# Moving one rounded copy of the activation from ScalarE to GpSimd in an attention and two-MLP kernel

## The chip, the cores and the metric

The kernel runs on one core of a Trainium2 chip. The metric is the device time of one execution in microseconds (us). The kernel before takes 946.75 us, the median of 3 runs (946.28 to 947.42). The core has five engines, each with its own queue worked off in order: TensorE (PE, with its weight loads shown as PEld), VectorE (DVE), ScalarE (ACT), GpSimd (POOL) and SyncE (SP), which issues the transfers.

## The reference

Attention with a window of 128 positions (4 batches, 8 heads, 576 positions, 64 dimensions a head), whose result, as 2304 tokens of 512 numbers, goes through two MLPs of inner width 2048:

```
scores = q k^T / 8 - slope_h * |i - j|,  only for 0 <= i - j < 128
x  = softmax(scores) v                          # 2304 x 512
h  = x @ w_in                                   # first MLP
g  = h where h >= 1, 0 where h <= -1, else (h + 1)^2 / 4
x2 = g @ w_out
h  = x2 @ w_in2                                 # second MLP
g  = h * clip(h + 3, 0, 6) / 6
out = g @ w_out2
```

## The kernel before, in words

[...] So that accuracy is kept, every operand is split into a high part (the value rounded to fp32r) and a low part (what the rounding left), and a product is three matmuls: low by high, high by low, high by high. `split_hi` (line 150) makes the high part on an engine that its first argument names, `split_lo` (line 158) the low part by a subtraction. The weights come as 64-bit numbers and are turned into f32 on the chip by `Weights.conv1` to `conv3`: on ACT (lines 194 and 198 and the cast), POOL (line 197, the sign) and DVE (lines 205 and 212 and the subtraction).

The first MLP runs over blocks of tokens: three of 256 (N1), then four of 384. A block goes through 16 chunks f of the inner width. One chunk is `first` (12 matmuls into a bank h, line 659), `activate` (lines 688 to 692: DVE clips h, ACT squares, DVE takes the larger, then high and low part of g) and, two chunks later, `second` (12 matmuls that read g, line 701). In `second` the first of each three matmuls reads the high part of g, the second the low part. Blocks 0 and 1 go in halves: chunks 0 to 7 of block 0, 0 to 7 of block 1, then 8 to 15 of each; block 2 goes whole.

Attention runs between these chunks, one step of up to 128 queries per `tick`. For the first four units of tokens the scores are made in f32 (transposes at lines 469 and 470, products with v at line 506, x at line 531), for the later ones with split operands: `prep` makes kh, kl, qs (line 393 on POOL) and vs (line 159 on POOL), the probabilities are scaled on POOL (line 450), and POOL puts the transposed ones under two masks (line 488). Scores are matmuls at line 411, and DVE takes their minimum at line 441.

What runs on PE, DVE, ACT and POOL here is not in the order of the program text: the framework's scheduler orders each engine's queue from its own estimate of times, save where `tc.issue_after` binds an instruction. SP's queue keeps the order of the text. From the later part of the second MLP on, all queues keep the text's order.

In `activate` of the first MLP the engine of the high part is `HI["g"]`, which is "act": a cast at line 152. The low part is on POOL until the last block, which takes DVE.

## Time and profile before

| | |
|---|---|
| median of 3 runs | 946.75 us (946.28 to 947.42) |
| profiled execution, its own time | 946.02 us |
| its span, first to last instruction | 944.3 us |
| PE busy, PEld busy | 928.5 us (98%), 875.5 us (93%) |
| DVE busy | 659.4 us (70%) |
| ACT busy | 535.6 us (57%) |
| POOL busy | 306.8 us (32%), nearly all of it in the first half |
| granted clock of TensorE | 1.00 over the whole span |

Busy time is the time in which an engine executes something, a mean over stages that are limited by different things. POOL's 32% of the span is 80% and more of some stretches and nothing in others, so the rows below are taken by stretch. Idle time of an engine is put down to what ended it. PE's matmuls overlap, and one that is shown with 0.28 us holds the engine only until the next one starts.

### The profile page before, as it was taken

The numbers are of one execution on the slowest core, as the hardware profiler recorded it, in microseconds if no ns is written. First come the engines' busy times: TensorE is split into PE (matmuls) and PEld (weight loads), VectorE is DVE, ScalarE is ACT, GpSimd is POOL, SyncE is SP. The second block draws the span as 40 slices with busy tenths as digits, with TensorE's granted clock in tenths as the row PEclk, the third lists the DMA queues.
The fourth block names the chain that finished last, engine by engine and source line by source line (L and its number), as shares of the span: only waits on it lengthen the run. The fifth ranks groups of instructions, "written<-read, shape, count | busy, mean of one in ns | idle before, by whom it ended". The sixth has DMA issues, their size and how long they took to land.

```text
span 944.3 us, 17237 instructions
## 1 busy us (share of the span) xinstructions
PE 928.5 (98%) x5683; PEld 875.5 (93%) x5683; DVE 659.4 (70%) x1750; ACT 535.6 (57%) x1349; POOL 306.8 (32%) x575
## 2 busy tenths in 40 slices
PE   8899999999999999999999999999999999999998
PEld 6799999999999999999999999999999888898987
DVE  6998975786677677767656899958557777644443
ACT  6998854676667566666635786535333334423233
POOL 3243845787668676777710000000000000000000
PEclk9999999999999999999999999999999999999999
DMA  8858322232222212322017771004264654543431
GB/s 256 240 178 264 111 89 88 68 86 67 73 64 72 79 46 62 89 75 62 1 55 270 266 237 55 1 23 167 81 210 170 232 174 146 169 124 114 123 112 67
DMA packets 95337, 114.90 MB, mean 122 GB/s; under 512 B 8848, under 2 KB 73616, under 8 KB 95248
## 3 DMA queue, kind: packets, MB, share of 16 engines
q1 hardware_dynamic: 95248, 113.80, 38.3%
q8 instruction: 45, 0.74, 0.3%
q14 instruction: 44, 0.36, 0.1%
HBM read 88.60 MB, written 25.17 MB: 120 GB/s over the span
## 4 chain that ended last, share of the span: by engine, by line
PE 89%; DVE 5%; ACT 2%; DMA 2%; issue 1%; POOL 1%; SPq 0%; ACTq 0%; DVEq 0%; POOLq 0%
PE h L659 26%; PE acc L760 21%; PE acc L701 18%; PE y L1249 7%; PE x L1249 5%; PE s L411 4%; PE r L554 3%; PE t L470 2%; PE r L506 2%; DMA rawa<-w_in 1%; DVE r L688 1%; DVE kl L391 1%; DVE r L690 1%; DVE x L159 1%; DMA kw<-kT 1%
## 5 line engine op out<-in xcount | busy, mean ns | idle before, releaser
L659 PE MATMUL h<-x,wa 128*128 128x384 f32 (+1 forms) x1344 | 231.0, 317 | 1.4 <-DVE r L690 0.9
L701 PE MATMUL acc<-g,wa 128*128 128x384 f32 (+1 forms) x1344 | 227.4, 315 | 0.4 <-POOL g L159 0.4
L760 PE MATMUL acc<-wb,g 128*128 128x512 f32 x861 | 222.2, 393 | 0.0
L659 PEld LDWEIGHTS h<-x,wa 128*128 128x128 f32 x1344 | 206.8, 189 | 4.3 <-DVE r L690 3.4
L701 PEld LDWEIGHTS acc<-g,wa 128*128 128x128 f32 x1344 | 206.3, 189 | 0.7 <-POOL g L159 0.6
L760 PEld LDWEIGHTS acc<-wb,g 128*128 128x128 f32 x861 | 159.4, 188 | 24.9
L152 ACT CAST g<-r 128x384 fp32r<-128x384 f32 (+1 forms) x208 | 101.6, 489 | 71.4 <-DVE r L1196 37.6
L159 POOL TENSOR_TENSOR g<-r,g 128x256 fp32r<-128x256 f32 (+1 forms) x96 | 92.5, 964 | 67.7 <-ACT g L152 54.8
L689 ACT ACTIVATE r<-r 128x384 f32<-128x384 f32 (+1 forms) x112 | 53.5, 479 | 81.3 <-DVE r L688 81.0
L159 DVE TENSOR_TENSOR g<-r,g 128x384 fp32r<-128x384 f32 x112 | 62.4, 557 | 41.9 <-ACT g L152 41.6
L688 DVE TENSOR_SCALAR r<-h 128x384 f32<-128x384 f32 (+1 forms) x112 | 55.4, 495 | 44.0 <-PE h L659 37.3
L488 POOL TENSOR_SCALAR_AFFINE_SELECT tt<-dist 128x256 fp32r<-128x256 f32 (+1 forms) x176 | 76.9, 458 | 13.9 <-DVE dist L483 13.8
L690 DVE TENSOR_TENSOR r<-h,r 128x384 f32<-128x384 f32 (+1 forms) x112 | 55.8, 499 | 30.3 <-ACT r L689 28.4
L659 PE MATMUL h<-x,wb 128*128 128x384 f32 x384 | 72.5, 336 | 0.0
L659 PEld LDWEIGHTS h<-x,wb 128*128 128x128 f32 x384 | 68.2, 188 | 2.6
L445 ACT ACTIVATE p<-p,sm 128x128 f32<-128x128 f32 (+2 forms) x134 | 57.3, 430 | 20.9 <-DVE sm L441 20.5
L1194 ACT ACTIVATE r<-u 128x384 f32<-128x384 f32 x32 | 16.9, 527 | 56.2 <-DVE u L1258 56.2
L554 PEld LDWEIGHTS r<-tt,vs 128*128 128x128 f32 x304 | 44.7, 189 | 3.2 <-issue 1.4
L393 POOL TENSOR_TENSOR qs<-qr,qs 128x256 fp32r<-128x256 f32 (+2 forms) x64 | 39.4, 616 | 24.9 <-ACT qs L390 13.3
L554 PE MATMUL r<-tt,vs 128*128 128x128 f32 (+3 forms) x304 | 44.3, 262 | 1.4 <-POOL tt L488 0.9
L470 PE MATMUL t<-ident,p 128*128 128x128 f32 x134 | 38.4, 288 | 0.5 <-ACT tt L152 0.5
L1249 PE MATMUL y<-wb,w 128*128 128x384 f32 x192 | 38.7, 336 | 0.0
(161 smaller groups left out, 1554.6 us busy)
## 6 DMA issues: line engine op xcount, KB each, us to landing
w<-wd SPq DMA_DIRECT2D x88, 256.0 KB, 2.7
rawa<-w_in SPq DMA_DIRECT2D x16, 512.0 KB, 5.3
rawa<-w_out SPq DMA_DIRECT2D x16, 512.0 KB, 5.4
rawb<-w_in SPq DMA_DIRECT2D x16, 512.0 KB, 3.8
rawb<-w_out SPq DMA_DIRECT2D x16, 512.0 KB, 4.7
wd<-sum SPq DMA_DIRECT2D x32, 256.0 KB, 2.1
wd<-wb SPq DMA_DIRECT2D x24, 256.0 KB, 2.8
out<-o SPq DMA_DIRECT2D x17, 256.0 KB, 2.3
```

The costliest lines, as they stand in the source:

```text
L152: nc.scalar.copy(hi, x)
L159: engines[eng].tensor_tensor(out=lo, in0=x, in1=hi.bitcast(F32), op=ALU.subtract)
L445: nc.scalar.activation(out=pt[:, :nk], in_=pt[:, :nk], func=AF.Exp, bias=sm[:, 0:1], scale=-1.0, accum_out=None if u.whole else sm[:, 1:2])
L470: nc.tensor.transpose(ps[:, 1, :], pt[:, P:] if u.whole and has_prev else pt[:, :P], ident)
L488: nc.gpsimd.affine_select(out=u.tt[:, :, s0 + s, :m], in_=both, compare_op=ALU.is_ge, fill=0.0, base=-1 + s, pattern=[[0, 2], [sign, m]], ...
L554: nc.tensor.matmul(u.r[:, qo:qo + nq], u.vs[:, j, c, :, :].rearrange("p a d -> p (a d)"), u.tt[:, part].rearrange("p s q -> p (s q)")[:, s ...
L659: nc.tensor.matmul(ps[:, :n], self.W.w_in(a, c, f), self.x_chunk(x, b, c, n), start=(k == 0), stop=(k == 3 * KC - 1))
L688: nc.vector.tensor_scalar(out=r[:, :n], in0=ps[:, :n], scalar1=-1.0, scalar2=1.0, op0=ALU.max, op1=ALU.min)
L690: self.larger = nc.vector.tensor_tensor(out=r[:, :n], in0=ps[:, :n], in1=r[:, :n], op=ALU.max)
L701: nc.tensor.matmul(acc[i][:, o * n:(o + 1) * n], self.W.w_out(a, f)[:, e * P:(e + 1) * P], g[:, b, :n], start=(first and k == 0 and o == 0 ...
L760: nc.tensor.matmul(acc[t][:, :DM], g[:, b, tg * P:(tg + 1) * P], self.W.w_out(a, f), start=(first and k == 0), stop=(last and k == 2))
L1249: nc.tensor.matmul(ps[:, :N2], w[:, a, c * P:(c + 1) * P], self.x.operand(k, c, b), start=(start and n == 0), stop=(n == 5), skip_group_ch ...
```

## The change

In `Mlp1.activate`, where the block has 256 tokens, the high part of g is made by POOL and no longer by ACT. `split_hi` does this on POOL as a multiplication by 1 twice in one instruction (`tensor_scalar`, line 154). Blocks of 384 tokens and the second MLP stay as they are. There are 48 such chunks (3 blocks of 16).

```
-            split_hi(HI["g"], g[:, 0, :n], r[:, :n])
+            split_hi("pool" if n == N1 else HI["g"], g[:, 0, :n], r[:, :n])
             split_lo(LO[self.g_lo], g[:, 1, :n], r[:, :n], g[:, 0, :n])
```

```
def split_hi(eng, hi, x):
    if eng == "act":
        nc.scalar.copy(hi, x)
    elif eng == "pool":
        nc.gpsimd.tensor_scalar(out=hi, in0=x, scalar1=1.0, scalar2=1.0, op0=ALU.mult, op1=ALU.mult)
```

As the scheduler orders the queues, other instructions move as well. PE's queue at the first chunk of g (acc_721 and acc_722 are the banks of block 0's second product, wa_397 and wa_494 weights, s scores, p and t probabilities before and after their transpose):

```order
 L411 MATMUL s_1_549<-kw_106,qw_107 128x256
 L659 MATMUL h<-x,wa_494 128x256 x12
-L701 MATMUL acc_721<-g,wa_397 128x256 x5
+L701 MATMUL acc_721<-g,wa_397 128x256 x2
 L469 MATMUL t_0_564<-ident,p_115 128x128
 L470 MATMUL t_0_564<-ident,p_115 128x128
+L701 MATMUL acc_721<-g,wa_397 128x256
 L411 MATMUL s_0_572<-kw_106,qw_107 128x256
+L701 MATMUL acc_721<-g,wa_397 128x256
 L469 MATMUL t_1_580<-ident,p_113 128x128
 L470 MATMUL t_1_580<-ident,p_113 128x128
 L701 MATMUL acc_721<-g,wa_397 128x256
```

Attention's transposes and scores have moved ahead of most of the products that read g. PE's queue differs in this way up to the end of the first half of block 1 and at two more places in the second half of block 0; behind these it is the same.

POOL's queue at the end of the first half of block 1 (rawa are weights whose sign is made, qs and vs operands of the attention; L154 is the new copy):

```order
 L197 TENSOR_SCALAR rawa_1218<-rawa_1218 128x1024
 L159 TENSOR_TENSOR g<-r,g 128x256
 L197 TENSOR_SCALAR rawa_1277<-rawa_1277 128x1024
+L159 TENSOR_TENSOR vs_1729<-vr_103,vs_1729 128x3x64
+L154 TENSOR_SCALAR g<-r 128x256
 L159 TENSOR_TENSOR g<-r,g 128x256
 L393 TENSOR_TENSOR qs_1724<-qr_1508,qs_1724 128x256
-L159 TENSOR_TENSOR vs_1729<-vr_103,vs_1729 128x3x64 x2
+L159 TENSOR_TENSOR vs_1729<-vr_103,vs_1729 128x3x64
 L197 TENSOR_SCALAR rawa_1349<-rawa_1349 128x1024
+L154 TENSOR_SCALAR g<-r 128x256
 L159 TENSOR_TENSOR g<-r,g 128x256
```

Two copies have come in between the weight rawa_1218 and the last g shown; a third stands directly ahead of rawa_1218. One of the two subtractions for vs has moved ahead of a g.

DVE's queue at the same place (L690 is the larger of h and the square, which ends r, the input of the copy; the others are passes over weights):

```order
 L205 SCALAR_TENSOR_TENSOR ma_1702<-ma_1702,rawa_1277 128x1024
 L688 TENSOR_SCALAR r<-h 128x256
 L159 TENSOR_TENSOR wa_1699<-ma_1615,wa_1699 128x1024
+L690 TENSOR_TENSOR r<-h,r 128x256
 L212 ISA ma_1702<-rawa_1277,ma_1702 128x2048
-L690 TENSOR_TENSOR r<-h,r 128x256
 L688 TENSOR_SCALAR r<-h 128x256
```

The end of r for the last chunk of block 1's first half has moved ahead of the pass at line 212.

POOL's queue in block 2, at a head whose qs is made late (tt_3285 are masked probabilities, p_115 probabilities that are scaled):

```order
-L159 TENSOR_TENSOR vs_3067<-vr_103,vs_3067 128x2x64 x2
+L159 TENSOR_TENSOR vs_3067<-vr_103,vs_3067 128x2x64
+L154 TENSOR_SCALAR g<-r 128x256
+L159 TENSOR_TENSOR vs_3067<-vr_103,vs_3067 128x2x64
 L159 TENSOR_TENSOR g<-r,g 128x256
 L488 AFFINE_SELECT tt_3285<-dist 128x2x128 x2
+L393 TENSOR_TENSOR qs_3306<-qr_3177,qs_3306 128x256
 L450 TENSOR_SCALAR p_115<-p_115,sm_0_3295 128x128
-L393 TENSOR_TENSOR qs_3306<-qr_3177,qs_3306 128x256
```

The copy has come in ahead of the low part of g, and qs has moved ahead of the scaling.

## Rows read from the trace of the kernel before

**Rows 1.** Stretches: length, then busy us of the engines, clock, DMA

```profile
core 0: us, PE busy (x) PEld busy (x) DVE busy (x) ACT busy (x) POOL busy (x), PEclk, DMA share, GB/s
40.00:83.00 43.00, 42.55 (x345) 41.21 (x344) 39.13 (x109) 40.10 (x87) 18.32 (x26) 1.00 0.57 175
83.00:107.00 24.00, 23.57 (x197) 23.13 (x197) 21.89 (x51) 22.12 (x48) 13.28 (x14) 1.00 0.72 240
107.00:133.00 26.00, 26.00 (x221) 26.00 (x220) 23.79 (x56) 17.55 (x44) 16.99 (x19) 1.00 0.24 74
133.00:160.00 27.00, 27.00 (x229) 26.92 (x228) 14.21 (x52) 12.85 (x40) 14.08 (x26) 1.00 0.36 109
160.00:228.00 68.00, 67.41 (x556) 65.86 (x556) 51.56 (x199) 46.77 (x165) 54.06 (x110) 1.00 0.26 70
```

**Rows 2.** Longest waits of PE, 40 to 228 us: total, times, longest

```profile
PE t L469 <- DVE x L159: 0.4, 1, 0.4
PE acc L701 <- POOL g L159: 0.4, 1, 0.4
```

**Rows 3.** Groups by shape, ACT and POOL, whole span: busy us, mean ns

```profile
L152 ACT CAST g<-r 128x256 fp32r<-128x256 f32 x48 | 19.5, 405 | 9.7 <-DVE r L690 8.5 <-PE s L411 0.9
...
L488 POOL TENSOR_SCALAR_AFFINE_SELECT tt<-dist 128x256 fp32r<-128x256 f32 x144 | 64.7, 470 | 13.9 <-DVE dist L483 13.8
...
L197 POOL TENSOR_SCALAR rawa<-rawa 128x1024 f32<-128x1024 f32 x16 | 23.6, 1475 | 39.5 <-ACT ma L194 22.2 <-DMA qw<-qT 8.8 <-DMA kw<-kT 4.6
...
L142 POOL TENSOR_SCALAR dist<-rel 128x256 bf16<-128x256 f32 x8 | 3.2, 406 | 0.3
```

**Rows 4.** Timeline of ACT at 97 us: start, duration, [idle before]

```profile
97.34 0.40 ACT L152 CAST g<-r 128x256 fp32r<-128x256 f32 x1
97.64 0.46 ACT L445 ACTIVATE p<-p,sm 128x192 f32<-128x192 f32 x1
...
99.82 1.20 ACT L194 ACTIVATE ma<-rawa 128x1024 f32<-128x1024 f32 x1 [0.22 <-DVE wa L159]
```

**Rows 5.** Longest wait of all engines, 25 to 230 us: total, times, longest

```profile
POOL g L159 <- ACT g L152: 27.9, 22, 3.0
```

**Rows 6.** Timeline of POOL at the first g

```profile
37.44 1.31 POOL L197 TENSOR_SCALAR rawa<-rawa 128x1024 f32<-128x1024 f32 x1 [3.91 <-DMA rawa<-w_in]
39.25 1.46 POOL L159 TENSOR_TENSOR g<-r,g 128x256 fp32r<-128x256 f32 x1 [0.49 <-ACT g L152]
```

**Rows 7.** Timeline of POOL at the end of block 1's first half

```profile
101.10 1.51 POOL L197 TENSOR_SCALAR rawa<-rawa 128x1024 f32<-128x1024 f32 x1 [0.70 <-ACT ma L194]
...
103.27 2.12 POOL L197 TENSOR_SCALAR rawa<-rawa 128x1024 f32<-128x1024 f32 x1
...
109.77 2.12 POOL L197 TENSOR_SCALAR rawa<-rawa 128x1024 f32<-128x1024 f32 x1
111.85 1.70 POOL L159 TENSOR_TENSOR g<-r,g 128x256 fp32r<-128x256 f32 x1
```

**Rows 8.** Timeline of PE at the products that read this g

```profile
113.69 1.68 PE L701 MATMUL acc<-g,wa 128*128 128x256 f32 x12
115.21 0.28 PE L659 MATMUL h<-x,wa 128*128 128x256 f32 x1
```

**Rows 9.** Timeline of DVE ahead of that

```profile
96.25 0.42 DVE L690 TENSOR_TENSOR r<-h,r 128x256 f32<-128x256 f32 x1 [0.42 <-ACT r L689]
```

**Rows 10.** Timelines of POOL and PE at a late qs in block 2

```profile
208.48 0.73 POOL L159 TENSOR_TENSOR g<-r,g 128x256 fp32r<-128x256 f32 x1
...
210.33 0.38 POOL L450 TENSOR_SCALAR p<-p,sm 128x128 f32<-128x128 f32 x1 [0.16 <-DVE sm L449]
210.67 0.74 POOL L393 TENSOR_TENSOR qs<-qr,qs 128x256 fp32r<-128x256 f32 x1
...
211.47 0.33 PE L411 MATMUL s<-kh,qs 128*128 128x128 f32 x1
```

**Rows 11.** Timelines of POOL and DVE where both read SBUF

```profile
43.95 1.17 POOL L197 TENSOR_SCALAR rawa<-rawa 128x1024 f32<-128x1024 f32 x1 [3.24 <-ACT ma L194]
...
49.34 2.21 POOL L197 TENSOR_SCALAR rawa<-rawa 128x1024 f32<-128x1024 f32 x1 [3.51 <-ACT ma L194]
...
49.32 1.21 DVE L212 CUSTOM_DVE_ANT_0 ma<-rawa,ma 128x2048 uint16<-128x2048 uint16 x1
```

**Rows 12.** Timeline of PE before the first g

```profile
38.12 0.70 PE L411 MATMUL s<-kw,qw 128*128 128x256 f32 x2 [1.09 <-DVE sm L441]
```

## The prediction

> **What bounds the kernel now.** I read the busy time by stretch first, because the change touches only the blocks of 256 tokens, whose copies of g lie between 38 and 229 us. In each stretch from 40 us on TensorE (PE) is busy for nearly all of it: it is idle for 0.45, 0.43, 0.00, 0.00 and 0.59 us, 1.47 us of 188 [rows 1]. [...] So PE bounds this part, the change takes nothing off PE, and what it can win there is first of all that 1.47 us. What it can lose is not bounded in that way: any new wait of PE comes out at the end, since the stretches behind are full too.

> Second, the helpers in the same rows. From 40 to 83 us ACT is busy for 40.10 of 43 us and DVE for 39.13; POOL only for 18.32. From 160 to 228 us it is the other way round: POOL has 54.06 of 68 us, ACT 46.77. The change moves work from ACT to POOL, which is welcome in the first stretch and unwelcome in the last.

> Third, the waits of PE: the two longest after 40 us are 0.4 us for DVE's x and 0.4 us for POOL's g [rows 2]. Neither is for the cast on ACT that the change removes.

> **The change, part by part.**

> *Removed:* 48 casts on ACT, of 405 ns [rows 3], 19.4 us of busy time. ACT starts its next instruction before a cast has ended: the one at 97.34 lasts 0.40, its successor starts at 97.64 [rows 4], so a cast takes 0.30 us of ACT's queue, 14.4 us in all.

> *Added:* 48 copies on POOL. The trace has no copy from f32 to fp32r there. The nearest rows are the same instruction on as many elements with a bf16 result, 406 ns, and a select on as many elements with an fp32r result, 470 ns; the upper end is the same instruction on four times as many elements, 1475 ns [rows 3]. I take 0.45 us, between the two of the right size: 21.6 us. In the unblocked case I see no reason for less than 0.41.

> *What hides it:* before its 48 subtractions POOL stood idle 22 times, for 27.9 us, until ACT's cast had ended [rows 5]. There the copy runs in a gap that is gone anyway, 0.45 in place of 0.41 and one hand-over fewer. The other 26 times it did not wait for ACT, so the copy is added to its queue. What follows is where that queue is tight.

> *First g, at 40 us.* PE waits 0.4 us for it [rows 2]. POOL is held until 38.75 by a weight's sign (37.44 + 1.31) [rows 6], and the subtraction starts at 39.25. A copy from 38.75 of 0.45 us lets it start at 39.20, and saves the hand-over: -0.05, call it -0.1 us at most. In the changed order PE has only two products of that g ahead of the transposes instead of five, so a late g holds up the attention a little less or the same.

> *End of block 1's first half, 101 to 114 us.* This is the tightest place. POOL works from 101.10 without any idle to the end of the subtraction at 113.55 (111.85 + 1.70) [rows 7]. The 12 products that read this g start at 113.69 and the next ones at 115.21 [rows 8], so each takes 0.13 us; the second is the first that reads the low part, and is due at 113.82. Slack: 0.27 us. By the changed POOL order one copy comes ahead of the weight at 101.10, where POOL had been idle for 0.70 us and which hides it, and two copies come between that weight and this subtraction; half of a pair of subtractions for vs goes ahead of one g, which moves nothing in the total. Two copies of 0.45 are 0.90, less the slack 0.27: 0.63 us late. Against it stands a lead: POOL's start at 101.10 follows ACT's weight pass of 99.82 [rows 4], that follows DVE, and DVE had lost 0.42 us at 96.25 waiting for ACT's square [rows 9]. The removed casts ahead of it give back one spacing, 0.30. Term: +0.3 us. Its bounds: 0 (the lead is larger, ACT being freed of 13 casts since 40 us) and +2.6 us (below).

> Behind the subtraction POOL has a qs of the attention and the next g. In the changed order DVE makes that g's maximum ahead of a weight pass and no longer behind it, so I put no second wait there.

> *Block 2, 160 to 228 us.* 16 copies of 0.45 are 7.2 us, and POOL has 13.9 us idle (68 - 54.06) [rows 1]; it stays below 91%. The one tight place that I find is the qs that ends at 211.41 (210.67 + 0.74) and is read by scores at 211.47 [rows 10]. The copy ahead of the g at 208.48 would push it by 0.45. But in the changed order this qs stands ahead of the scaling of p, so it gains 0.38 and the 0.16 us that POOL waited for DVE there. Term: 0, bounds -0.4 (the chain of DVE and ACT runs ahead because ACT is freed) and +0.9 (two copies late).

> The sum is -0.1 + 0.3 + 0 = +0.2 us. The profiled execution took 946.02 us, a span of 944.3 and 1.7 around it, so 946.2 by its own time. The median of the runs is 946.75, 0.73 above the profiled one; I forecast **947.0 us**, no measurable change. For this kernel 0.2%, or 1.9 us, is about what a measurement can tell from none.

> [...] The trace shows that copies on POOL can cost more than 0.45. A weight's sign on POOL lasts 1.17 us at 43.95 and 2.21 us at 49.34, where DVE had just begun, at 49.32, an addition of two tiles in SBUF; that addition lasted 1.21 us [rows 11]. So POOL waited for DVE, about 1.0 us. From 103 to 114 us POOL's weight passes take 2.12 us and the subtractions 1.70 again [rows 7].

> [...]

> **Rivals.**

> 1. *Slower: POOL's queue at 101 to 114 us with blocked copies.* If each of the two copies is held by DVE as the weight's sign was, it takes 0.45 + 1.0 = 1.45 us; two are 2.9, less the slack 0.27: +2.6 us, 949.4 us. It decides from 1.25 us a copy on (2 x 1.25 - 0.27 - 0.3 = 1.9). For it: all four rows of that stretch are lengthened. Against it: a copy is short and can fall beside DVE's reads from PSUM, and a blocked copy partly takes over the blocking of the subtraction behind it.

> 2. *Faster: ACT was the hidden pacer of 40 to 107 us.* ACT is busy for 62.22 of 67 us there [rows 1], and the 13 casts in them give back 3.9 us. Weights and exponentials come earlier, and PE's gaps close. PE's own idle time allows -1.5 us, 945.3; weight loads on PE (PEld) are idle for 4.9 us over the same stretches, and half of that would be -2.4 us, 944.3. Against it: PE shows hardly a wait to close.

> 3. *Slower: the new order on PE.* From the first g on attention is issued earlier among the products. If the chain DVE, ACT, PE of the scores is not ready, PE waits; between 24 and 40 us one such wait is 1.09 us [rows 12]. Two more of them are +2.2 us, 949.0 us. Against it: the products that are pushed back have to be done anyway and their g gets later need, and DVE's share is as before.

> That the change does nothing isn't a rival: the POOL order shows all the copies.

> **Chances.** Forecast 0.56, first rival 0.17, second 0.17, third 0.10. Faster than 0.2% takes the second rival in its larger size and something of the unknown in block 2: 0.16. Slower takes most of the first and third: 0.24. Within 0.2%: 0.60. The range runs from PE's idle time all won (945.3) to the price of the slow rivals (949.0 and 949.4; I take 949.2); outside I leave some of each.

> **What would show it.** Right: POOL copies of 0.41 to 0.5 us, PE's idle time from 40 to 228 us within 1 us of 1.47, products of block 1's last g starting less than 1 us late for POOL, and the stretches behind 228 us unchanged in length. The first rival shows as copies over 1.2 us between 101 and 114 us and as a wait of PE for POOL's g of over 1 us. The second shows as block 2 starting over 1.5 us earlier with DVE or ACT less far behind. The third shows as waits of PE for DVE's maxima or ACT's exponentials between 40 and 107 us. I am wrong altogether if the difference arises behind 230 us, where no engine's order moves.

## The result and the profile after

The changed kernel took 952.32 us (median of 4 runs, 950.29 to 952.92), the kernel before 946.74 us in the same measurement (946.28 to 947.42). The ratio is 1.0055, with a 95% interval of 1.0043 to 1.0068. That is 5.6 us slower, where 947.0 us was forecast, and outside the range given.

The profiled execution of the changed kernel is its fastest, 950.29 us with a span of 948.6 and a mean clock of 1.000; the other three have 0.997 or 0.998. That difference turns out to be a part of the loss. First the stretches, in the columns of [rows 1].

```profile
core 0: us, PE busy (x) PEld busy (x) DVE busy (x) ACT busy (x) POOL busy (x), PEclk, DMA share, GB/s
40.00:83.00 43.00, 42.54 (x336) 40.74 (x336) 38.67 (x104) 37.91 (x77) 19.81 (x33) 1.00 0.58 179
83.00:107.00 24.00, 22.99 (x194) 22.68 (x194) 22.47 (x49) 20.64 (x41) 16.68 (x20) 1.00 0.76 247
107.00:133.00 26.00, 23.73 (x199) 23.34 (x199) 22.12 (x49) 15.61 (x38) 22.95 (x24) 1.00 0.18 54
133.00:160.00 27.00, 27.00 (x229) 26.91 (x228) 15.61 (x58) 9.44 (x29) 16.66 (x33) 1.00 0.42 127
160.00:228.00 68.00, 67.59 (x563) 66.34 (x562) 51.03 (x197) 41.27 (x146) 59.99 (x127) 1.00 0.25 70
```

PE's idle time has gone from 1.47 to 4.15 us: 0.46, 1.01, 2.27, 0 and 0.41. The new idle time lies between 83 and 133 us, and in the third stretch POOL has gone from 16.99 to 22.95 of 26 us. Block 2, from 160 us on, has lost nothing. The waits of PE from 40 to 228 us name the same place (total us, times, longest; compare [rows 2]):

```profile
PE acc L701 <- POOL g L154: 1.8, 1, 1.8
PE s L411 <- DVE sm L441: 1.2, 2, 1.0
PE acc L701 <- POOL g L159: 0.9, 2, 0.4
```

PE's timeline shows them. Before, PE had no wait for g here [rows 8]; the products that read the last g but one of this half (g 14, counting every call from 0) now wait 1.85 us for its copy and another 0.43 for its low part.

```profile
103.75 0.59 PE L411 MATMUL s<-kw_kh,qw 128*128 128x192 f32 x2 [1.01 <-DVE sm L441]
...
118.02 0.38 PE L701 MATMUL acc<-g,wa 128*128 128x256 f32 x1 [1.85 <-POOL g L154]
118.83 1.58 PE L701 MATMUL acc<-g,wa 128*128 128x256 f32 x11 [0.43 <-POOL g L159]
120.25 1.60 PE L659 MATMUL h<-x,wa 128*128 128x256 f32 x12
```

POOL's timeline shows why. It answers to [rows 7]:

```profile
103.51 0.41 POOL L154 TENSOR_SCALAR g<-r 128x256 fp32r<-128x256 f32 x1 [1.39 <-DVE rec L518]
103.88 2.13 POOL L197 TENSOR_SCALAR rawa<-rawa 128x1024 f32<-128x1024 f32 x1
...
110.28 0.39 POOL L154 TENSOR_SCALAR g<-r 128x256 fp32r<-128x256 f32 x1
...
115.52 2.08 POOL L197 TENSOR_SCALAR rawa<-rawa 128x1024 f32<-128x1024 f32 x1
117.57 0.39 POOL L154 TENSOR_SCALAR g<-r 128x256 fp32r<-128x256 f32 x1
118.05 0.73 POOL L159 TENSOR_TENSOR g<-r,g 128x256 fp32r<-128x256 f32 x1
```

The first copy, that of g 12, stands at the head of the queue and waits 1.39 us for its r, with a weight's sign behind it (the row names the DVE instruction that ended last; r itself ends one earlier, at 103.42); from there POOL has no wait until 120.8 us, and the sign of weight 15 (2.08 us) is done just ahead of the copy for which PE waits. The three copies of this chain are short, 0.39 to 0.41 us; what is long here are signs and other passes. The groups by shape say the same of the copies over the whole span (busy us, mean ns; compare [rows 3]): 469 ns in the mean.

```profile
L154 POOL TENSOR_SCALAR g<-r 128x256 fp32r<-128x256 f32 x48 | 22.5, 469 | 25.0 <-DVE r L690 16.0 <-DVE sm L448 2.2 <-PE acc L701 2.0
```

To place the loss I number the products of L659 in the order of PE and compare the start of the same one with that of the kernel before ("lag"). The executions already differ when the first block begins, by 0 to 1.25 us at instructions that are the same in both programs, so each lag is also given less that start.

| run | at 23 us | at 96 us | at 119 us | at 228 us | 119 us less start | 228 us less start |
|---|---|---|---|---|---|---|
| changed kernel | 1.13 | 1.78 | 5.04 | 4.43 | 3.91 | 3.30 |
| the same once more | 0.54 | 1.29 | 6.02 | 5.40 | 5.48 | 4.86 |

So 0.65 to 0.75 us are lost by 96 us, 3.3 to 4.7 us between 96 and 119 us, and 0.6 us come back in block 2. The first figure is hardly more than two executions can differ by: the run with the copies in block 2 alone (below), whose queues up to 170 us are those of the kernel before, has 0.55 by 96 and 0.57 by 119 us. And up to 119 us PE's queue differs, so that the lag at 96 us compares fairly only kernels with the same order. The spans at the end differ from that before (944.3) by 4.3 and 5.8 us, so behind 228 us hardly anything is added.

### The profile page after: what moved, and what is told of

Same layout as the page of the kernel before. It is cut to its first block, busy times and chain, and to the rows that moved or that the text cites. A ratio compares the mean times of both kernels' runs of the same rounds, so it can differ in the third digit from the quotient of the medians.

```text
span 948.6 us, 17242 instructions
## 1 busy us (share of the span) xinstructions
PE 930.4 (98%) x5683; PEld 876.7 (92%) x5683; DVE 661.5 (70%) x1750; ACT 521.1 (55%) x1301; POOL 329.0 (35%) x623
## 4 chain that ended last, share of the span: by engine, by line
PE 87%; DVE 4%; POOL 3%; ACT 2%; DMA 2%; issue 2%; SPq 0%; ACTq 0%; POOLq 0%; DVEq 0%
PE h L659 26%; PE acc L760 21%; PE acc L701 18%; PE y L1249 7%; PE x L1249 5%; PE s L411 3%; PE r L554 3%; PE t L470 2%; DMA rawa<-w_in 1%; POOL rawa L197 1%; PE r L506 1%; DVE r L688 1%; DMA rawa<-w_out 1%; DVE ma L205 1%; DVE kl L391 1%
## 5 line engine op out<-in xcount | busy, mean ns | idle before, releaser
L659 PE MATMUL h<-x,wa 128*128 128x384 f32 (+1 forms) x1344 | 230.2, 317 | 1.3 <-DVE r L690 0.9
L659 PEld LDWEIGHTS h<-x,wa 128*128 128x128 f32 x1344 | 206.7, 189 | 4.3 <-DVE r L690 3.3
L152 ACT CAST g<-r 128x384 fp32r<-128x384 f32 x160 | 81.8, 512 | 59.6 <-DVE r L1196 37.6
L690 DVE TENSOR_TENSOR r<-h,r 128x384 f32<-128x384 f32 (+1 forms) x112 | 55.8, 498 | 29.4 <-ACT r L689 27.5
L659 PE MATMUL h<-x,wb 128*128 128x384 f32 x384 | 72.5, 336 | 0.0
L659 PEld LDWEIGHTS h<-x,wb 128*128 128x128 f32 x384 | 68.2, 188 | 2.6
```

The source lines that it names most:

```text
L152: nc.scalar.copy(hi, x)
L659: nc.tensor.matmul(ps[:, :n], self.W.w_in(a, c, f), self.x_chunk(x, b, c, n), start=(k == 0), stop=(k == 3 * KC - 1))
L690: self.larger = nc.vector.tensor_tensor(out=r[:, :n], in0=ps[:, :n], in1=r[:, :n], op=ALU.max)
```

## The experiments

Three theories. **Theory 1:** POOL's queue at the end of block 1's first half. **Theory 2:** the new order of PE's instructions, which the scheduler made because the copies moved. **Theory 3:** every copy costs something, wherever it stands. The kernel before was run beside all of them: 946.76 to 946.82 us.

### Where the copies cost

The condition of the copy was narrowed; copies are counted in the order of the program (0 to 7 are the first half of block 0, 8 to 15 the first half of block 1, 16 to 31 the second halves, 32 to 47 block 2).

```diff
-            split_hi("pool" if n == N1 else HI["g"], g[:, 0, :n], r[:, :n])
+            self.k = getattr(self, "k", -1) + 1; split_hi("pool" if n == N1 and self.k >= 32 else HI["g"], g[:, 0, :n], r[:, :n])
```

In all of these the scheduler orders the queues anew, so more than the copies can move. In the others the condition is `self.k < 32`, `12 <= self.k < 16` and, below, `self.k >= 16`, `not 12 <= self.k < 16` and `self.k != 12`.

The changed kernel once more:

> The changed kernel once more, nothing altered. All theories: 950 to 953 us, as before. What it is for: if the loss sits in GpSimd's queue at the end of block 1's first half (theory 1), its profile shows again a TensorE wait of 1.5 to 2.5 us for GpSimd's g near 118 us, and the wait of about 1 us for VectorE's maximum near 104 us; if those two waits were an accident of one execution, they are gone or elsewhere while the time stays. The lag of about 1.1 us that the first profile of the changed kernel picked up at 5 to 7.5 us, where both programs are the same, should be gone if it is a difference between executions.

951.87 us (4 runs), ratio 1.0055 (1.0040 to 1.0070). The two waits are there again, 1.84 and 1.00 us. But now the clock falls behind the longer one. By stretches, in the columns of [rows 1]:

```profile
119.00:122.00 3.00, 3.00 (x16) 3.00 (x15) 2.52 (x5) 0.99 (x4) 2.69 (x4) 0.50 0.44 121
122.00:123.00 1.00, 1.00 (x9) 1.00 (x9) 0.06 (x1) 0.00 (x0) 1.00 (x3) 0.79 0.31 103
```

From 119 to 122 us the granted clock is 0.50, and 0.79 in the microsecond behind. PE's timeline has the price: 2.18 in place of 1.58 us for the rest of the products of g 14, and 2.54 in place of 1.60 for the twelve behind, together 1.5 us.

```profile
117.51 0.39 PE L701 MATMUL acc<-g,wa 128*128 128x256 f32 x1 [1.84 <-POOL g L154]
118.31 2.18 PE L701 MATMUL acc<-g,wa 128*128 128x256 f32 x11 [0.42 <-POOL g L159]
120.29 2.54 PE L659 MATMUL h<-x,wa 128*128 128x256 f32 x12
```

Block 2 alone:

> GpSimd makes the rounded copy in block 2 alone (16 of 48 copies). Theory 1 (GpSimd's queue at the end of block 1's first half): nothing lost, 946.0 to 946.9 us. Theory 2 (the new order of TensorE's instructions): also nothing, 946.7 us, since TensorE's order is that of before here. Theory 3 (each copy costs about 0.12 us wherever it stands): a third of the loss, about 948.6 us.

946.41 us (10 runs), ratio 0.9996 (0.9987 to 1.0006). No loss: theory 3 falls.

Blocks 0 and 1 alone:

> GpSimd makes the rounded copy in blocks 0 and 1 alone (32 of 48 copies). Theory 1 and theory 2: the whole loss or a little more, 952 to 953 us (the first profile gives back 0.6 us in block 2, which this kernel would not get). Theory 3 (each copy costs the same): two thirds of the loss, about 950.5 us.

953.22 us (4 runs), ratio 1.0064 (1.0049 to 1.0079), the whole loss and a little more; its profile, too, has the clock at 0.50 behind the wait for g 14.

The last four of block 1's first half alone:

> GpSimd makes the rounded copy for the last four hidden chunks of block 1's first half alone (g 12 to 15), TensorE's order being that of before; in the order of GpSimd's instructions the copy and low part of g 14 now stand ahead of the sign of the weight that held them up. Theory 1 in its narrow form (what costs is the weight's sign in front of g 14, not the copies): 946.5 to 947.5 us, no TensorE wait above 1 us for GpSimd near 118 us. Theory 1 in its wide form (four copies in that stretch are enough to hold TensorE up): 948 to 949.5 us. Theory 2 (TensorE's order): 946.7 us. Theory 3: 947.2 us.

948.68 us (10 runs), ratio 1.0020 (1.0011 to 1.0030): four copies cost 1.9 us under PE's old order. Theory 1 in its narrow form falls, and so does theory 2 as the only cause. Without a weight's sign in front, the copy of g 14 was simply long itself, 1.37 us, and the low parts wait behind the copies. The copy of g 12 costs too: it waits 1.58 us for its r with two signs behind it, DVE waits 0.80 us for the first of these, and PE 0.98 us for DVE, where it had waited 0.43. POOL, DVE, then PE:

```profile
101.25 0.40 POOL L154 TENSOR_SCALAR g<-r 128x256 fp32r<-128x256 f32 x1 [1.58 <-DVE rec L518]
...
103.30 2.24 POOL L197 TENSOR_SCALAR rawa<-rawa 128x1024 f32<-128x1024 f32 x2
...
114.14 1.37 POOL L154 TENSOR_SCALAR g<-r 128x256 fp32r<-128x256 f32 x1
115.60 0.73 POOL L159 TENSOR_TENSOR g<-r,g 128x256 fp32r<-128x256 f32 x1
```

```profile
104.47 2.15 DVE L205 SCALAR_TENSOR_TENSOR ma<-ma,rawa 128x1024 uint32<-128x1024 uint32 x1 [0.80 <-POOL rawa L197]
```

```profile
108.41 0.33 PE L469 MATMUL t<-ident,p 128*128 128x128 f32 x1 [0.98 <-DVE x L159]
...
116.38 1.58 PE L701 MATMUL acc<-g,wa 128*128 128x256 f32 x11 [0.43 <-POOL g L159]
```

From the second halves on:

> GpSimd makes the rounded copy from the second halves of blocks 0 and 1 on (copies 16 to 47); TensorE's order is that of the kernel before. All theories but the third: no loss, and the gain of 0.3 to 0.6 us of block 2: 946.0 to 946.6 us. Theory 3 (each copy costs the same): 950.4 us.

946.18 us (11 runs), ratio 0.9996 (0.9988 to 1.0005): 32 of the 48 copies cost nothing.

### What in the queue decides

All but copies 12 to 15:

> GpSimd makes all rounded copies but those of g 12 to 15 (ScalarE makes these four, as before the change); TensorE's order is exactly that of the changed kernel. Theory 1 (GpSimd's queue between 102 and 118 us makes TensorE wait 2.3 us, after which the clock falls for some 3 us, about 1.5 us more): the waits for g 14 and the low clock near 120 us are gone, what stays is the new order's 0.9 us at 97 us and about 0.5 us at 104 to 108 us, less the 0.6 us won in block 2: 947.3 to 948.3 us. Theory 2 (the new order of TensorE carries the loss): 951 to 952.5 us. Theory 3 (each copy costs the same): 44 of 48 copies, about 951.5 us.

950.23 us (4 runs), ratio 1.0039 (1.0025 to 1.0052). All three theories miss: with the four copies back on ACT, 3.5 us of loss stay. The sign of weight 15 still stands ahead of the low part of g 14, and PE waits for that:

```profile
117.97 1.58 PE L701 MATMUL acc<-g,wa 128*128 128x256 f32 x11 [1.59 <-POOL g L159]
```

The sign of weight 15 behind g 14 (base: the changed kernel):

```diff
-                nc.gpsimd.tensor_scalar(out=sign, in0=sign, ...)
+                with (tc.issue_after(lows[{15: 14}[f]].ins) if f in {15} else ExitStack()): nc.gpsimd.tensor_scalar(out=sign, in0=sign, ...)
...
-            split_lo(LO[self.g_lo], g[:, 1, :n], r[:, :n], g[:, 0, :n])
+            lows.append(split_lo(LO[self.g_lo], g[:, 1, :n], r[:, :n], g[:, 0, :n]))
```

> The changed kernel with one instruction moved: GpSimd's sign of weight 15, which stands ahead of the copy of g 14, is placed behind the low part of g 14; the other engines keep their order, TensorE's above all. Theory 1: the TensorE wait of 1.85 us for g 14 is gone and with it the low clock near 120 us; 0.4 us waits for low parts stay, and g 15 comes about 0.5 us late in its place: 952.1 less 1.85 less 1.5 plus 0.5, about 949.2 us (948.5 to 950.0). Theory 2 (TensorE's order) and theory 3 (number of copies): no change, 951.5 to 952.5 us.

950.65 us (4 runs), ratio 1.0045 (1.0031 to 1.0058), 1.2 us below the repeat of the changed kernel, which the intervals of four runs each don't separate, and less than expected. The clock stays at 0.999 to 1.000. But the wait for the copy falls only from 1.85 to 0.78 us, since the copy, now first, takes 1.38 us. POOL, then DVE:

```profile
115.65 1.38 POOL L154 TENSOR_SCALAR g<-r 128x256 fp32r<-128x256 f32 x1
117.11 0.73 POOL L159 TENSOR_TENSOR g<-r,g 128x256 fp32r<-128x256 f32 x1
117.81 1.14 POOL L197 TENSOR_SCALAR rawa<-rawa 128x1024 f32<-128x1024 f32 x1
```

```profile
115.51 1.25 DVE L212 CUSTOM_DVE_ANT_0 ma<-rawa,ma 128x2048 uint16<-128x2048 uint16 x1
```

DVE had begun the weight pass of line 212 0.14 us earlier, as it had in the changed kernel 0.14 us ahead of the sign (115.38 against 115.52). What POOL issued next was about 1 us longer in both, a sign (2.08 against 1.14) or a copy (1.38 against 0.39): in these two traces it was the place in the queue that decided, not which pass stood there.

The copy of g 12 back on ACT:

> The changed kernel with one copy of 48 given back to ScalarE, that of g 12, which stood in GpSimd's queue for 1.39 us waiting for r ahead of a weight's sign; TensorE's order is that of the changed kernel. Theory 1: GpSimd's chain up to g 14 starts about 1.8 us earlier, so the wait of 1.85 us near 118 us falls to 0 to 0.5 us and the clock stays high: 948.5 to 949.5 us. Theory 1 in a narrower form (only the weight 15's sign matters, the queue ahead of it has slack): 951 to 952.5 us. Theory 2: no change, 951.5 to 952.5 us. Theory 3: 952.0 us.

952.14 us (4 runs), ratio 1.0055 (1.0040 to 1.0070): nothing won. With the head of the queue clear, POOL runs dry and waits for the next r:

```profile
108.39 0.41 POOL L154 TENSOR_SCALAR g<-r 128x256 fp32r<-128x256 f32 x1 [1.52 <-DVE r L690]
...
112.23 3.06 POOL L159 TENSOR_TENSOR vs<-vr,vs 128x192 fp32r<-128x192 f32 x2
115.26 1.37 POOL L154 TENSOR_SCALAR g<-r 128x256 fp32r<-128x256 f32 x1
116.60 1.10 POOL L197 TENSOR_SCALAR rawa<-rawa 128x1024 f32<-128x1024 f32 x1
117.68 0.72 POOL L159 TENSOR_TENSOR g<-r,g 128x256 fp32r<-128x256 f32 x1
```

In this kernel the chain begins at the copy of g 13, at 108.39, and ends at the low part of g 14. But the run doesn't take out the 1.39 us alone. The scheduler also put both passes for vs behind the copy of g 13, where the changed kernel has one of them ahead of it (at 108.75), and the sign of weight 15 between the copy and the low part of g 14. What the first copy's wait is worth with the rest of the queue held is not shown.

### Work and order apart

Two kernels separate what GpSimd does from what the scheduler made of it. A table of instruction numbers fixes the order of an engine; the tables were read from the two built programs.

```diff
+        impose(nc, tc)
...
+def impose(nc, tc):
+    by = {i.name: i for i in nc.cur_bb.bb.instructions}
+    for runs in ORDER:
+        order = [by[f"I-{a + k}"] for a, n in runs for k in range(n)]
+        for before, behind in zip(order, order[1:]):
+            tc.add_manual_dep(behind, before.name, ...)
```

The new work in the old order (base: the changed kernel):

> All 48 rounded copies on GpSimd as in the changed kernel, but TensorE, VectorE and ScalarE keep exactly the order of the kernel before (a table of numbers sets it; ScalarE's less its 48 copies), and GpSimd too, with each copy placed right ahead of its low part. This is the change without the scheduler's new order. If the new order carries most of the loss (theory 2): 946.2 to 947.5 us. If GpSimd's load and queue carry it (theory 1): 949 to 952 us, with TensorE waits for g between 104 and 122 us. Theory 3: 952 us.

949.66 us (9 runs), ratio 1.0025 (1.0016 to 1.0035). The work alone costs 2.9 us. Three executions took 947.8 to 948.2 us at a mean clock of 0.999 or 1.000, six took 949.6 to 950.4 at 0.997 or 0.998. The profiled one is of the first kind. Its POOL, DVE and PE:

```profile
101.19 1.52 POOL L197 TENSOR_SCALAR rawa<-rawa 128x1024 f32<-128x1024 f32 x1 [0.50 <-ACT ma L194]
102.67 0.40 POOL L154 TENSOR_SCALAR g<-r 128x256 fp32r<-128x256 f32 x1
...
106.77 1.41 POOL L154 TENSOR_SCALAR g<-r 128x256 fp32r<-128x256 f32 x1
...
110.66 3.06 POOL L159 TENSOR_TENSOR vs<-vr,vs 128x192 fp32r<-128x192 f32 x2
...
114.75 0.41 POOL L154 TENSOR_SCALAR g<-r 128x256 fp32r<-128x256 f32 x1
115.24 0.72 POOL L159 TENSOR_TENSOR g<-r,g 128x256 fp32r<-128x256 f32 x1
```

```profile
106.70 1.22 DVE L212 CUSTOM_DVE_ANT_0 ma<-rawa,ma 128x2048 uint16<-128x2048 uint16 x1
```

```profile
115.21 0.39 PE L701 MATMUL acc<-g,wa 128*128 128x256 f32 x1 [1.72 <-POOL g L154]
116.02 1.58 PE L701 MATMUL acc<-g,wa 128*128 128x256 f32 x11 [0.42 <-POOL g L159]
```

The low part of g 14 starts at 115.24 where it had started at 111.85 [rows 7], 3.4 us later: three copies, one of them long because DVE had begun a weight pass 0.07 us earlier, and longer passes for vs. Of the other passes between some are longer and some shorter than before, and together they come out nearly even. PE's lag goes from -0.44 to 2.23 us at this place, +2.7 us.

The new order with the old work (base: the kernel before):

> The other half of the square: ScalarE makes all the copies as before the change, but TensorE, VectorE and GpSimd (less the copies) stand exactly in the order of the changed kernel, and so does ScalarE's other work, its copies being placed by the scheduler. This is the new order without the change. If the new order carries most of the loss (theory 2): 949.5 to 951 us, with the excursion of 2.5 to 3.5 us in TensorE's lag at 65 to 80 us and a TensorE wait of about 1.6 us for GpSimd's low part near 118 us, behind the sign of weight 15. If GpSimd's load carries it (theory 1): 946.5 to 948 us. Theory 3: 946.8 us.

950.85 us (5 runs), ratio 1.0039 (1.0025 to 1.0052). The order alone costs 4.1 us, at a full clock in all runs (0.999 to 1.000). Here the wait behind weight 15's sign, expected at about 1.6 us, has shrunk to about 0.3: the twelve products of g 14 take 2.00 us where they took 1.68 [rows 8]. In its place PE waits at four others:

```profile
47.40 0.70 PE L411 MATMUL s<-kw_kh,qw 128*128 128x256 f32 x2 [0.70 <-DVE sm L441]
...
98.55 0.33 PE L469 MATMUL t<-ident,p 128*128 128x128 f32 x1 [0.39 <-DVE x L159]
104.78 0.59 PE L411 MATMUL s<-kw_kh,qw 128*128 128x192 f32 x2 [0.54 <-DVE sm L441]
107.12 0.41 PE L506 MATMUL r<-vr,tt 128*128 128x65 f32 x2 [0.45 <-issue]
...
117.64 2.00 PE L701 MATMUL acc<-g,wa 128*128 128x256 f32 x12
```

The four are together 2.1 us, where the kernel before has one such wait of 0.43 us [rows 2]; the rest I have not placed wait by wait. The medians side by side:

| | order of before | order of the changed kernel |
|---|---|---|
| copies on ACT | 946.8 | 950.9 |
| copies on POOL | 949.7 | 951.9 and 952.3 |

Both count, and they don't add up: 4.1 and 2.9 would be 7.0, and 5.1 to 5.6 were measured. The order costs less with the copies for which it was made: by 96 us it has lost 2.42 us (less start) alone, but 0.64 to 1.52 in the six profiles that have PE's new order and the copies up to there on POOL. The clock is the other part of the sum. At a full clock the new work in the old order takes 947.8 to 948.2 us, 1.0 to 1.4 above the kernel before; the rest of its 2.9 us is the clock. In the new order the copies then add nothing that shows: the lag at 119 us less start is 4.07 us with the order alone, and 3.91, 4.27 and 4.30 in the three full-clock profiles with order and copies (the changed kernel, the one with copies 12 to 15 on ACT, the one with weight 15's sign moved). With the clock down it is 5.48 to 5.94.

### The clock, and the queue without the four copies

Zeros in the wait, added to the kernel with the new work in the old order:

```diff
-            self.scores(u, ps, qo, ko, nk)
+            [keep_busy(ps, 2 * P) for _ in range(16) if (n, i) == (31, 0)]; self.scores(u, ps, qo, ko, nk)
```

> All copies on GpSimd in the order of the kernel before, as in the run that separated work from order (949.66 us median: 947.8 us in the executions with a mean clock of 1.000, 949.6 to 950.4 us in those with 0.997 or 0.998), with 16 matmuls of zeros (128 x 256, bf16) put in TensorE's queue ahead of the scores that stand before the wait for g 14, so that TensorE works through most of that wait of about 2 us. The zeros are overwritten by the scores. If the low clock follows from TensorE's idle stretch there: no execution below 0.999, median 947.6 to 948.2 us, although TensorE has 1.7 us more to do. If the low clock has another cause: again two groups and a median of 949.5 us or more. If the wait is not real idle time and the zeros add to the path: 951 us.

948.50 us (11 runs), ratio 1.0020 (1.0011 to 1.0029). No execution below 0.999, where six of nine had been at 0.997 or 0.998. The median is 1.2 us lower with 16 more matmuls in the queue, though 0.3 us above the range expected; the means differ by 0.6 us only, which so few runs don't separate. What is clear is the clock.

```profile
114.40 1.91 PE L125 MATMUL s<-zeros 128*128 128x256 bf16 x16
...
116.69 0.39 PE L701 MATMUL acc<-g,wa 128*128 128x256 f32 x1 [0.15 <-POOL g L154]
```

Six of nine executions without the zeros and none of eleven with them have the lower mean clock: here the fall of the clock follows from PE's idle stretch. Its size fits too: a mean clock of 0.998 over 948 us comes to 0.002 x 948 = 1.9 us, an estimate that counts the missing share of the clock as lost time, and about the distance between the two groups above.

The old order, and copies 12 to 15 on ACT:

> The order of the kernel before on all engines, 44 copies on GpSimd right ahead of their low parts, and the copies of g 12 to 15 on ScalarE at their old places. If the whole price of the work alone is GpSimd's queue at the end of block 1's first half: no wait for g near 115 us, no low clock, and what is left is the 0.4 us won in block 2 less the 0.3 us lost by 97 us: 946.2 to 946.9 us. If the copies cost wherever they stand: about 949.4 us.

946.61 us (11 runs), ratio 0.9997 (0.9988 to 1.0006). With 44 copies on POOL nothing is lost: the whole price of the work is the queue around g 12 to 15. Nothing measurable is won either. No version beat the kernel before by more than its interval; the lowest, with the copies from the second halves on, is 0.6 us below it.

## Why the prediction was wrong, point by point

*PE bounds this part, and any new wait comes out at the end:* right. PE's idle time rose by 2.7 us, and the lag stays to the end.

*A copy takes 0.45 us:* right, 0.469 in the mean of 48.

*First g, -0.1 us:* PE waits 0.45 us for its low part where it had waited 0.41; no gain, no loss.

*End of block 1's first half, +0.3 us:* **this is the step that failed.** It counted two copies of 0.45 us less a slack and a lead. In the changed kernel PE waits 1.85 and 0.43 us there. In the old order, where nothing else moves, the same place costs 2.7 us: three copies lie on the chain, one of them takes 1.41 us because DVE holds it up, and the passes for vs grow from 2.10 to 3.06. That is the first rival's size (+2.6) and nearly its mechanism; but the point was not whether two copies are blocked (in the changed kernel none of the three is). POOL has several passes in a row there, and several that began in a weight pass of DVE came out long, whichever they were (2.08 us for the sign at 115.52 in the changed kernel, 1.41 for the copy at 106.77 in the old order), so what is added to the queue is added to a chain with next to no slack. The lead of 0.30 us that was set against it did not come: in the old order the chain's first pass, a sign, starts at 101.19 where it had started at 101.10 [rows 7].

*The copy ahead of the weight is hidden in 0.70 us of idle time:* wrong in the changed order, where it waits 1.39 us with the weight's sign behind it. That this decided was my own first reading of the trace; the run without that copy won nothing, but it moved other passes as well, so what the wait is worth stays open.

*Block 2, 0 us:* no loss, as forecast, and a small gain, which was the lower bound. The lag falls by 0.6 us there in the changed kernel, in its repeat and with the copies in block 2 alone (5.04 to 4.43, 6.02 to 5.40, 1.82 to 1.23), a little more than the bound of -0.4. The gain goes with the copies: in the old order with them the lag falls by 0.4 (2.23 to 1.84), in the new order without them it rises by 0.3 (4.67 to 4.98).

*Second rival, ACT as the hidden pacer:* not so. With 44 casts off ACT and no new order the time is that of before.

*Third rival, PE's new order, 0.10:* real, and larger than its +2.2: 4.1 us alone. **This is the second step that failed:** the sum has no term for the new order, on the ground that the products pushed back have to be done anyway. Its sign shows as announced, a wait of 1.01 us at 103.75 for the row value that DVE takes at line 441 (a minimum).

*The clock:* in no term and no rival. A wait of some 2 us on PE was priced at 2 us; in most executions a lower clock followed (0.50 for about 3 us in the repeat) and cost another 1.5 to 1.9 us.

The rivals were set against each other, each with its own chance, as if one excluded the other. Queue and order came together and the clock came on top, and so the range, which ended at the price of one, was left.

What stays open: which of the moved rows on PE make the order's 4.1 us, beyond the 2.1 us of waits and the 0.3 shown, and which wait in block 2 gives the 0.6 us back.

## What to carry to other kernels

Before work is moved to an engine that looks idle on average, take the chain of its passes from its last idle moment to the moment when the bound engine needs the output, at the tightest place, and price each pass at the length that it has beside the other engines' passes (here 1.24 to 1.48 us for a copy that alone takes 0.41). Where a scheduler makes the order, changing an engine changes the order too: fix the old order and measure the two apart. And price a stall of TensorE in the middle of full work at more than its length: behind a wait of 1.84 us the clock fell here to 0.50 for about 3 us, which cost 1.5 us more, and with matmuls of zeros in the gap it stayed at 0.999 to 1.000 in eleven executions.

## What the runs showed of the hardware

Passes on POOL were up to about 1 us longer, whichever they were: 0.39 and 1.38 for the copy, 1.10 and 2.08 for a weight's sign, with lengths between (1.24 for the copy at 121.07 in the changed kernel). The copy shows when. In the changed kernel three of the 48 took more than 0.9 us: 1.38 at 51.11, 1.48 at 94.36 and 1.24 at 121.07. Each began while DVE was in a weight pass (lines 212, 205 and 159) and ended 0.26 or 0.27 us behind the end of that pass; so did the copies of 1.41 and 1.23 us in the new work in the old order (106.77, 118.26) and the one of 1.38 us with the sign moved. Of the other 45 one took 0.63 us (129.52, beside DVE's pass for kl at line 391) and the rest 0.39 to 0.42, among them the eleven that began while DVE was reading h or scores from PSUM (lines 688 and 441), with 0.39 to 0.41. When one pass was taken out of the way the next one met such a weight pass, so that the gain was less than what was removed (1.07 us of a 1.85 us wait, when a sign of 2.08 us was moved away).

At instructions that are the same in all programs, before 23 us, executions differed by up to 1.25 us; a single profiled execution against another says nothing about a difference of that size. Taking the start off narrowed this to about half a us (0.57 us at 119 us between two programs that are the same up to there).
